# A chunked attention feeding a top-2 expert layer, on one core: first loads and turns reordered, some copies moved between ACT and DVE, routing constants spread over three iterations

## The chip, the cores and the metric

The kernel runs on one core of a Trainium2 chip. A core has a matrix engine (PE, with its weight loads PEld), a vector engine (DVE), a scalar engine (ACT), a general engine (POOL) and a sync engine (SP). Each engine works through its own instructions in order and waits on semaphores that others raise. Loads are queued by an engine and carried by 16 DMA engines. The metric is the device time of one execution in microseconds; lower is better.

## The reference, cut to what matters

Attention works in chunks of 32 queries. Each chunk sees 8 memory keys, up to 16 keys to its left, its own 32 and up to 8 to its right. The rows of the result go through a router with two choices out of 8 experts, each expert being two matrix products with a ReLU between them.

```python
batch, n_heads, seq, head_dim = (4, 8, 768, 64)
chunk, left_ctx, right_ctx = (32, 16, 8)
for c in range(nc):
    k_full = np.concatenate([mem_k, k_ctx], axis=2)
    v_full = np.concatenate([mem_v, v_ctx], axis=2)
    scores = scale * np.matmul(q_c, k_full.transpose(0, 1, 3, 2))
    a = np.exp(scores - np.max(scores, axis=-1, keepdims=True))
    a = a / (np.sum(a, axis=-1, keepdims=True) + 1e-09)
    out[:, :, c_start:c_end] = np.matmul(a, v_full)
...
x = attn_out.transpose(0, 2, 1, 3).reshape(B * S, H * D)        # 3072 rows of 512
noisy_logits = x @ w_gate + np.log1p(np.exp(x @ w_noise)) * noise
top2 = np.argpartition(-noisy_logits, 2, axis=1)[:, :2]
...
h = np.maximum(x[mask] @ w1[e], 0.0)                            # 512 to 1024
out[mask] += top2_w[mask, k, None] * (h @ w2[e])                # 1024 to 512
```

## The kernel before

The attention part takes two heads at a time, a pair: 16 pairs (NPAIR), four of them (HP) for each of the 4 batches. Everything about one pair is a row of short steps, each a function of the pair's number:

- `load_qk(n)` and `load_v(n)` (L126, L134) bring a pair's q, k and v from memory, cast to bf16. All of them are queued on POOL, in program order. q and k have six buffers each (NQ), v has four (NV). A v buffer is cleared once at the start (L161, L166), as chunks at the sequence's ends leave parts of it unwritten. A v load is two transfers, one for each head (three where the first or last head is in it).
- `turn_pe(n, 0)` transposes q on PE (twelve transposes, L254) into one of three PSUM banks, which all transposes share in a ring, and ACT copies the result out (qT, L258). `turn_pe(n, 1)` does k; ACT copies it in two halves (kT, L264) into one of two buffers whose other halves were set to zero (L204).
- `scores_pe` (L273 to L283) multiplies q with the memory keys (mkT) and with the windows of k, into bankS.
- `max_dve` takes the row maxima (mx, L288) and subtracts them (sd, L290), both on DVE. `exp_act` (L295) exponentiates on ACT.
- `PT_pe` transposes the probabilities on PE, `PT_copy` (L307) copies them out on ACT, `PV_pe` (L314, L317) multiplies them with the memory values (memv) and with v, into bankO, and `mult_dve` (L328, L329) divides by the row sums on DVE.
- `xT_pe` transposes the finished rows and copies them out on ACT (xt, L342), and `logits_pe` (L350) multiplies them with the gate weights (wgn).

The order of the work is written by hand: a main loop over i runs PT, PV and the division for pair i - 1, maximum and exponential for pair i, the turns for pair i + 2, the transposes of rows for pair i - 2, and the scores for pair i + 1. It also queues the loads of q and k for pair i + 6 and of v for pair i + 3. So the text below says "iteration i" and means the stretch that begins with pair i's maximum. Ahead of the loop stand the turns of pairs 0 and 1 and the scores of pair 0.

From iteration 6 on, whenever four pairs make a batch complete, the steps of the router (`route`, a list of small functions, put into `pending`) are worked off two at a time, one in the middle and one at the end of each iteration (`steps(1)`). The router needs constants: ramps, identities and small masks, which `route_constants` (L218 to L232) makes on DVE, all of them in iteration 1. The memory keys are transposed by PE ahead of everything else (L241), with a 32x32 identity in fp32 that DVE copies (L194), and ACT copies the result to mkT (L243). At the start ACT holds nothing else but a table load and the issue of the memory keys.

After the loop come the last batch's router, gathers of rows by expert (L615), and the experts' products (`up`, L667; `down`, L683), whose results are scattered to the output (L695). That part is the same in both kernels.

Of the kernel before, what the change touches and what calls it, by code (L numbers as in the profile page):

```python
# [24 lines left out]
def kernel(  # L25
# [14 lines left out]
    nc = tc.nc  # L40
# [48 lines left out]
    def body():  # L89
# [32 lines left out]
        def load_qk(n):  # L122
            b, h0 = divmod(2 * n, H)
            qks[n] = [ap_.tile([128, 2, SJ * D], BF16, name=nm, bufs=NQ) for nm in ("qg", "kg")]
            for dst, src in zip(qks[n], (q, k)):
                nc.gpsimd.dma_start(out=dst, in_=src[b, h0:h0 + 2].rearrange("h (p j) d -> p h (j d)", p=128))  # L126
# [32 lines left out]
        OW = D + 2  # L159
        memv = ap_.tile([128, NPAIR, 2, OW], BF16, name="memv", bufs=1)  # L160
        nc.vector.memset(vbufs[0], 0.0)  # L161
        nc.vector.memset(memv, 0.0)
# [30 lines left out]
        ident = ap_.tile([32, 32], F32, name="ident", bufs=1)  # L193
        nc.vector.tensor_copy(ident, identb[:32, :32])  # L194
        onesb = const.tile([128, 128], BF16, name="onesb")
        nc.vector.memset(onesb, 1.0)
        neg = const.tile([128, 2, left_ctx], BF16, name="neg")
        nc.vector.memset(neg, NEG)
        mkT = ap_.tile([128, HP, B, 2, n_mem], BF16, name="mkT", bufs=1)
        nc.vector.memset(mkT, 0.0)  # L200
        kbufs = [ap_.tile([128, 2, S], BF16, name=f"kT{i}", bufs=1) for i in range(2)]
        for kb in kbufs:
            for hh in range(2):
                nc.vector.memset(kb[64 * (1 - hh):64 * (1 - hh) + 64, hh, :], 0.0)  # L204
# [10 lines left out]
        wgn = rp.tile([128, KP, 2 * E], BF16, name="wgn")  # L215

        def route_constants():
            nc.vector.tensor_copy(ramp, ramp_i)  # L218
            nc.vector.tensor_scalar(out=rampm, in0=ramp_i, scalar1=-128.0, scalar2=None, op0=Alu.add)
            nc.vector.tensor_copy(tokv[:, :NP // 2], tok_i[:, :NP // 2])  # L220
            nc.vector.tensor_scalar(out=tokv[:, NP // 2:], in0=tok_i[:, NP // 2:], scalar1=1.0, scalar2=None, op0=Alu.add)
            nc.vector.tensor_copy(step, step_i)
            nc.vector.memset(ones16, 1.0)
            nc.vector.tensor_copy(ident16, identb)
            for hh in range(2):
                nc.vector.tensor_copy(fold[:, hh, :], identb[:64, :64])
            nc.vector.memset(row0, 0.0)
            nc.vector.memset(row0[0:1, :], 1.0)
            for hh in range(2):
                nc.vector.memset(halfc[64 * hh:64 * hh + 64, :], float(hh))  # L230
                nc.vector.memset(pick[:, hh, :], float(hh))
            nc.vector.tensor_copy(wgn, wgn_f.rearrange("p k t e -> p k (t e)"))  # L232
# [6 lines left out]
        p_m = f32v(tr(), HP, B * n_mem)  # L239
        for hp in range(HP):  # L240
            nc.tensor.transpose(out=p_m[:, hp, :], in_=mk_nat[:, 2 * hp:2 * hp + 2, :].rearrange("p h d -> p (h d)"), identity=ident)  # L241
        for hh in range(2):
            nc.scalar.copy(mkT[64 * hh:64 * hh + 64, :, :, hh, :], p_m[64 * hh:64 * hh + 64].rearrange("p h (b m) -> p h b m", m=n_mem))  # L243


        st = [dict() for _ in range(NPAIR)]
        xrows = {}

        def turn_pe(n, x):
            src = qks[n][x]  # L250
            p_t = bf16v(tr(), SJ, 128)
            for j in range(SJ):
                for hh in range(2):
                    nc.tensor.transpose(out=p_t[64 * hh:64 * hh + 64, j, :], in_=src[:, hh, j * D:(j + 1) * D], identity=identb)  # L254
            p_t = p_t.rearrange("d j p -> d p j")
            if x == 0:
                dst = ap_.tile([128, 128, SJ], BF16, name="qT", bufs=2)
                nc.scalar.copy(dst, p_t)  # L258
                st[n]["qT"] = dst.rearrange("d p j -> d (p j)")
            else:  # L260

                for hh in range(2):
                    hs = slice(64 * hh, 64 * hh + 64)
                    nc.scalar.copy(kbufs[n % 2][hs, hh].rearrange("d (p j) -> d p j", j=SJ), p_t[hs])  # L264

        UB = BT // 2

# [18 lines left out]
        def max_dve(n):  # L286
            mx = ap_.tile([128, 2, BT], F32, name="mx")
            nc.vector.tensor_reduce(out=mx, in_=st[n]["ps"], axis=AX, op=Alu.max)  # L288
            sd = ap_.tile([128, 2, BT, CTX], F32, name="sd", bufs=1)
            nc.vector.tensor_tensor(out=sd, in0=st[n]["ps"], in1=mx.rearrange("p x (u o) -> p x u o", o=1).to_broadcast([128, 2, BT, CTX]), op=Alu.subtract)  # L290
            st[n]["sd"] = sd
# [10 lines left out]
                nc.tensor.transpose(out=p_p[:, u, :], in_=P[:, u, :, :], identity=identb)  # L302
            st[n]["p_p"] = p_p

        def PT_copy(n):
            PT = ap_.tile([128, BT, 128], BF16, name="PT", bufs=1)
            nc.scalar.copy(PT, st[n]["p_p"])  # L307
            st[n]["PT"] = PT

        def PV_pe(n):  # L310
# [543 lines left out]

        PT_pe(n - 1)
        max_dve(n)
        PT_copy(n - 1)
        PV_pe(n - 1)
        exp_act(n)
# [180 lines left out]
```

## Time and profile before

| | us |
|---|---|
| median of 3 runs | 334.99 |
| lowest and highest run | 334.16, 338.81 |
| the profiled execution, device time | 335.06 |
| its span, first to last instruction | 333.0 |
| PE, DVE, ACT, POOL busy | 271.9, 163.0, 149.5, 227.4 |

The profile is one execution, with a start and a duration in us for each instruction, counted from the start of the span; 2.06 us of the execution lie outside it. In a timeline row the numbers are start and duration, then engine, line, operation, written tile and read tile, shapes, the count of instructions merged into the row, and in brackets how long the engine stood idle before it and what released it. In a window row they are the length of the stretch and the busy time of each engine in it. For a group of instructions they are the busy sum, the mean duration in ns, and the idle time ahead of it. For a load they are its size and the time from issue to landing. Most of the idle time of ACT and DVE in the expert part is theirs to have, since PE is the busy engine there.

### The profile page before, as it was taken

Reading aid. Unit: us, or ns where it says so; the run is one execution under the profiler, and the core shown is the slowest. Engines: PE = TensorE matmul, PEld = TensorE weight load, DVE = VectorE, ACT = ScalarE, POOL = GpSimd, SP = SyncE. Lnnn points to the kernel's source line nnn. Section 1 sums busy time; section 2 is a strip of 40 time slices with the busy share of each in tenths; the row PEclk is TensorE's granted clock in tenths of the full one; section 3 lists DMA queues with packets and bytes.
Section 4 is the critical chain, followed back from the end, with each engine's and each line's share of the span. In section 5 each row is a group of like instructions: output and inputs, shape, how many; then the busy total and the mean of one; then the engine's idle time right before and its main releaser. Section 6 shows DMA issues by size and latency. Waiting matters only on the chain.

```text
span 333.0 us, 7629 instructions
## 1 busy us (share of the span) xinstructions
PE 271.9 (82%) x3065; PEld 173.2 (52%) x3085; DVE 163.0 (49%) x363; ACT 149.5 (45%) x295; POOL 227.4 (68%) x220
## 2 busy tenths in 40 slices
PE   0776777786766768969999999999999999999920
PEld 0655565565655557536546464564554556455410
DVE  7556668869998684313434342342342434234200
ACT  1687997788673644313343423323422324333100
POOL 8996878554652256774878686887886888675480
PEclk9978997989875799999999999999999999999975
DMA  9999999999997998899989999999999979979293
GB/s 106 157 150 186 171 162 165 213 140 151 237 213 160 335 362 291 132 220 248 172 162 196 210 204 200 211 174 198 190 208 214 183 122 173 196 86 134 33 130 49
DMA packets 99846, 60.30 MB, mean 181 GB/s; under 512 B 65056, under 2 KB 84768, under 8 KB 99808
## 3 DMA queue, kind: packets, MB, share of 16 engines
q0 software_dynamic: 82160, 50.63, 106.8%
q1 hardware_dynamic: 14272, 8.98, 9.2%
q10 hardware_dynamic: 3376, 0.16, 1.0%
q8 instruction: 26, 0.43, 0.5%
q14 instruction: 12, 0.10, 0.1%
HBM read 65.07 MB, written 23.27 MB: 265 GB/s over the span
## 4 chain that ended last, share of the span: by engine, by line
PE 45%; DVE 15%; issue 13%; DMA 8%; ACT 8%; POOL 8%; POOLq 1%; DVEq 0%; ACTq 0%
PE bankE L683 13%; PE bankE L667 12%; POOL out_dram L695 7%; PE bankT L667 6%; DMA out_dram<-ys,idx_h 4%; DMA w2t<-in_moe_w_dram 3%; ACT kT L264 3%; DVE xrow L329 2%; PE bankO L314 2%; PE bankO L317 2%; PE bankT L638 2%; ACT PT L307 2%; PE bankT L254 2%; DVE mx L288 2%; DVE Rn L454 2%
## 5 line engine op out<-in xcount | busy, mean ns | idle before, releaser
L695 POOL DMA_INDIRECT out_dram<-ys,idx_f x40 | 63.1, 1577 | 24.0 <-issue 16.3
L667 PEld LDWEIGHTS <-w1t 128*128 128x128 bf16 x576 | 55.2, 99 | 36.4 <-issue 5.0
L683 PE MATMUL bankE<-w2t,htf 128*128 128x512 bf16 x278 | 64.7, 379 | 0.5
L615 POOL DMA_INDIRECT xl<-x_rows,idx_f x48 | 50.0, 1041 | 22.2 <-issue 10.1
L694 DVE TENSOR_SCALAR ys<-bankE,gt 128x512 f32<-128x512 f32 (+1 forms) x32 | 21.9, 684 | 63.8 <-PE bankE L683 50.8
L667 PE MATMUL bankE<-xTf,w1t 128*128 128x320 bf16 (+1 forms) x250 | 51.3, 338 | 1.7 <-ACT xTf L640 1.4
L692 ACT ACTIVATE ys<-bankE,gt 128x512 f32<-128x512 f32 x24 | 16.5, 688 | 65.5 <-PE bankE L683 51.7
L134 POOL DMA_DIRECT2D vp<-in_v_dram x34 | 33.3, 986 | 15.5 <-PE bankO L317 4.4
L683 PEld LDWEIGHTS <-htf 128*128 128x128 bf16 x288 | 27.4, 97 | 29.9 <-issue 0.2
L652 DVE TENSOR_SCALAR htf<-bankE 128x512 bf16<-128x512 f32 (+1 forms) x32 | 18.9, 592 | 28.3 <-PE bankE L667 28.3
L650 ACT ACTIVATE htf<-bankE 128x512 bf16<-128x512 f32 (+1 forms) x32 | 16.5, 517 | 27.5 <-PE bankE L667 26.4
L264 ACT COPY kT<-bankT 64x768 bf16<-64x768 bf16 x32 | 25.3, 791 | 6.3 <-PE bankT L254 6.1
L667 PE MATMUL bankT<-xTf,w1t 128*128 128x320 bf16 (+1 forms) x128 | 27.8, 339 | 0.0
L683 PE MATMUL bankE<-w2t,hts 128*128 128x512 bf16 x92 | 21.5, 379 | 2.8 <-DMA w2t<-in_moe_w_dram 2.6
L638 PEld LDWEIGHTS <-xl 128*128 128x128 bf16 (+1 forms) x224 | 15.5, 99 | 12.4 <-issue 4.7
L638 PE MATMUL bankT<-identb,xl 128*128 128x128 bf16 (+1 forms) x224 | 20.3, 218 | 0.8 <-ACT xt L342 0.5
L667 PE MATMUL bankE<-xTs,w1t 128*128 128x256 bf16 (+1 forms) x128 | 18.8, 290 | 2.2 <-ACT xTs L640 1.4
L314 PE MATMUL bankO<-memv,PT 128*128 128x132 bf16 x96 | 10.3, 258 | 12.3 <-ACT PT L307 8.0
L288 DVE TENSOR_REDUCE mx<-bankS 128x12 f32<-128x768 f32 x16 | 15.2, 953 | 8.9 <-PE bankS L283 8.8
L652 DVE TENSOR_SCALAR htf<-bankT 128x512 bf16<-128x512 f32 (+1 forms) x16 | 9.5, 592 | 15.3 <-PE bankT L667 14.4
L290 DVE TENSOR_TENSOR sd<-bankS,mx 128x768 f32<-128x768 f32 x16 | 15.3, 958 | 1.9 <-ACT xt L342 0.5
L295 ACT ACTIVATE P<-sd 128x768 bf16<-128x768 f32 x16 | 13.6, 850 | 5.3 <-DVE sd L290 5.3
(182 smaller groups left out, 449.3 us busy)
## 6 DMA issues: line engine op xcount, KB each, us to landing
w1t<-in_moe_w_dram POOLq DMA_DIRECT2D x8, 1024.0 KB, 12.4
w2t<-in_moe_w_dram POOLq DMA_DIRECT2D x8, 1024.0 KB, 11.2
out_dram<-zt SPq DMA_DIRECT2D x3, 2048.0 KB
vp<-in_v_dram POOLq DMA_DIRECT2D x30, 168.0 KB, 7.8
qg<-in_q_dram POOLq DMA_DIRECT2D x16, 192.0 KB, 7.8
kg<-in_k_dram POOLq DMA_DIRECT2D x16, 192.0 KB, 8.2
x_rows<-xrow SPq DMA_DIRECT2D x2, 792.0 KB, 9.0
x_rows<-xrow SPq DMA_DIRECT2D x1, 768.0 KB, 8.3
```

The costliest lines, as they stand in the source:

```text
L134: nc.gpsimd.dma_start(out=vp[p0 + j:p0 + j + nj, c:c + m, hh, :], in_=bass.AP(v.tensor, v.offset + (hd * S + c * chunk + j - left_ctx) * D ...
L264: nc.scalar.copy(kbufs[n % 2][hs, hh].rearrange("d (p j) -> d p j", j=SJ), p_t[hs])
L288: nc.vector.tensor_reduce(out=mx, in_=st[n]["ps"], axis=AX, op=Alu.max)
L314: nc.tensor.matmul(out=pv[:, u // UB, u % UB], lhsT=PT[:, u, :], rhs=memv[:, n], start=(u % UB == 0), stop=False, skip_group_check=True)
L615: nc.gpsimd.indirect_dma_start(out=xl, out_offset=None, in_=xd[:upto], in_offset=bass.IndirectOffsetOnAxis(ap=idx[:, c:c + 1], axis=0), bo ...
L638: nc.tensor.transpose(out=p_t[:, kp, :w], in_=xl[:w, kp * 64:(kp + 1) * 64].bitcast(BF16), identity=identb[:w, :w])
L650: nc.scalar.activation(out=dst, in_=src, func=Act.Relu)
L652: nc.vector.tensor_scalar(out=dst, in0=src, scalar1=0.0, scalar2=None, op0=Alu.max)
L667: nc.tensor.matmul(out=h[:, :hi - lo], lhsT=W1[e][:, kp, f * 128:(f + 1) * 128], rhs=xTs[s][:, kp, lo:hi], start=(kp == 0), stop=(kp == KP ...
L683: nc.tensor.matmul(out=y, lhsT=ht[:, f, o:o + w], rhs=W2[e][:, f, :], start=(f == 0), stop=(f == FB - 1))
L694: nc.vector.tensor_scalar(out=ys[:, :wide], in0=y[:, :wide], scalar1=gate, scalar2=None, op0=Alu.mult)
L695: ins = nc.gpsimd.indirect_dma_start(out=rows, out_offset=bass.IndirectOffsetOnAxis(ap=idx, axis=0), in_=ys[:, :wide], in_offset=None, bou ...
```

## The change

The order of the first instructions is new on every engine:

- POOL queues q and k of pair 2 ahead of v of pair 0, makes the router's index tables ahead of the loads of pair 3, and queues v of pairs 1 and 2 behind q and k of pairs 3 and 4. v of pair 3 moves out of the start altogether: iteration 0 queues it, after q and k of pair 6.
- DVE clears one v buffer, then the memory keys' tile and the halves of the two kT buffers, then makes the identity and the other small constants, and only then clears memv and the last v buffer. The second and third v buffer are cleared by ACT, which copies the first one's zeros.
- PE turns q of pair 0 first, then the memory keys, then k of pair 0 and q of pair 1; the scores of pair 0 stand ahead of k of pair 1. For pairs 0 and 2 one of the two halves of kT is copied by DVE instead of ACT.

In the loop, the maximum and the subtraction become two functions, and in iterations 1 to 6 DVE copies PT between them (pairs 0 to 5); from iteration 7 on ACT copies PT as before. The router's constants become six entries of `pending`, which iterations 0 to 2 work off, two in each.

```diff
         nc.vector.memset(vbufs[0], 0.0)
+        mkT = ap_.tile([128, HP, B, 2, n_mem], BF16, name="mkT", bufs=1)
+        nc.vector.memset(mkT, 0.0)
+        kbufs = [ap_.tile([128, 2, S], BF16, name=f"kT{i}", bufs=1) for i in range(2)]
+        for kb in kbufs:
+            for hh in range(2):
+                nc.vector.memset(kb[64 * (1 - hh):64 * (1 - hh) + 64, hh, :], 0.0)
+        ident = ap_.tile([32, 32], F32, name="ident", bufs=1)
+        nc.vector.tensor_copy(ident, identb[:32, :32])
...
-        for vb in vbufs[1:]:
-            nc.vector.memset(vb, 0.0)
+        flat = lambda t: t.rearrange("p c h d -> p (c h d)").bitcast(F32)
+        for vb in vbufs[1:3]:
+            nc.scalar.copy(flat(vb), flat(vbufs[0]))
+        nc.vector.memset(vbufs[3], 0.0)
+        load_qk(2)
         load_v(0)
...
-        load_qk(2)
-        load_v(1)
-        load_qk(3)
...
+        load_qk(3)
+        load_v(1)
+        load_qk(4)
         load_v(2)
-        load_qk(4)
-        load_v(3)
         load_qk(5)
...
         def route_constants():
...
+            return [
+                (lambda: V.tensor_copy(wgn, wgn_f.rearrange("p k t e -> p k (t e)")), lambda: V.tensor_copy(step, step_i)),
+                (lambda: V.tensor_copy(ramp, ramp_i), lambda: V.memset(ones16, 1.0)),
+                (lambda: V.tensor_scalar(out=rampm, in0=ramp_i, scalar1=-128.0, scalar2=None, op0=Alu.add), lambda: V.tensor_copy(ident16, identb)),
...
+                (halves,),
+                (folds,)]
...
-        def turn_pe(n, x):
+        def turn_pe(n, x, both=False):
...
-                    nc.scalar.copy(kbufs[n % 2][hs, hh].rearrange("d (p j) -> d p j", j=SJ), p_t[hs])
+                    (nc.vector.tensor_copy if both and hh else nc.scalar.copy)(kbufs[n % 2][hs, hh].rearrange("d (p j) -> d p j", j=SJ), p_t[hs])
...
-        def PT_copy(n):
+        def PT_copy(n, copy=nc.scalar.copy):
             PT = ap_.tile([128, BT, 128], BF16, name="PT", bufs=1)
-            nc.scalar.copy(PT, st[n]["p_p"])
+            copy(PT, st[n]["p_p"])
...
-        for n in range(2):
-            turn_pe(n, 0)
-            turn_pe(n, 1)
-            if n == 0:
-                scores_pe(0)
+        turn_pe(0, 0)
+        memory_keys()
+        turn_pe(0, 1, True)
+        turn_pe(1, 0)
+        scores_pe(0)
+        turn_pe(1, 1)
+        pending.extend(route_constants())
         for i in range(NPAIR - 1):
...
             max_dve(i)
-            if i >= 1:
+            if 1 <= i <= HP + 2:
+                PT_copy(i - 1, nc.vector.tensor_copy)
+            sub_dve(i)
+            if i > HP + 2:
                 PT_copy(i - 1)
...
-                turn_pe(i + 2, 1)
+                turn_pe(i + 2, 1, i == 0)
...
-            if 1 <= i <= NPAIR - NV:
+            if i <= NPAIR - NV:
                 load_v(i + NV - 1)
-            if i == 1:
-                route_constants()
```

`memory_keys` is the old code of L241 and L243 as a function, `folds` and `halves` the old lines for the masks, `sub_dve` the old L290.

More of the change, by code (lines that the diff above doesn't have):

```diff
@@ L161, in body @@
         nc.vector.memset(vbufs[0], 0.0)
+        mkT = ap_.tile([128, HP, B, 2, n_mem], BF16, name="mkT", bufs=1)
[6 more added lines that the diff above has]
+        nc.vector.tensor_copy(ident, identb[:32, :32])
+        onesb = const.tile([128, 128], BF16, name="onesb")
+        nc.vector.memset(onesb, 1.0)
+        neg = const.tile([128, 2, left_ctx], BF16, name="neg")
+        nc.vector.memset(neg, NEG)
         nc.vector.memset(memv, 0.0)
@@ L186, in body @@
         nc.gpsimd.affine_select(out=tie, in_=tie, compare_op=Alu.is_gt, fill=0.0, base=0, pattern=[[1, E], [-1, E]], channel_multiplier=0)
+        load_qk(3)
+        load_v(1)
+        load_qk(4)
         load_v(2)
-        load_qk(4)
-        load_v(3)
         load_qk(5)
[L193 to L204, printed above, removed]
         ramp = const.tile([128, 128], F16, name="ramp")
@@ L217, in route_constants, with halves, folds @@
         def route_constants():
[L218 to L232, printed above, removed]
+            V = nc.vector
+            def halves():
+                for hh in range(2):
+                    V.memset(halfc[64 * hh:64 * hh + 64, :], float(hh))
+                    V.memset(pick[:, hh, :], float(hh))
+            def folds():
+                for hh in range(2):
+                    V.tensor_copy(fold[:, hh, :], identb[:64, :64])
+                V.memset(row0, 0.0)
+                V.memset(row0[0:1, :], 1.0)
+            return [
+                (lambda: V.tensor_copy(wgn, wgn_f.rearrange("p k t e -> p k (t e)")), lambda: V.tensor_copy(step, step_i)),
+                (lambda: V.tensor_copy(ramp, ramp_i), lambda: V.memset(ones16, 1.0)),
+                (lambda: V.tensor_scalar(out=rampm, in0=ramp_i, scalar1=-128.0, scalar2=None, op0=Alu.add), lambda: V.tensor_copy(ident16, identb)),
+                (lambda: V.tensor_copy(tokv[:, :NP // 2], tok_i[:, :NP // 2]),
+                 lambda: V.tensor_scalar(out=tokv[:, NP // 2:], in0=tok_i[:, NP // 2:], scalar1=1.0, scalar2=None, op0=Alu.add)),
+                (halves,),
+                (folds,)]
         seen = rp.tile([128, E], F16, name="seen")
@@ L237, in body @@
         tabs = [rp.tile([128, NC_], F32, name=f"tab{i}") for i in range(2)]
[L239 to L243, printed above, removed]
         st = [dict() for _ in range(NPAIR)]
         xrows = {}
-        def turn_pe(n, x):
+        def turn_pe(n, x, both=False):
             src = qks[n][x]
@@ L263, in turn_pe, with memory_keys @@
                     hs = slice(64 * hh, 64 * hh + 64)
-                    nc.scalar.copy(kbufs[n % 2][hs, hh].rearrange("d (p j) -> d p j", j=SJ), p_t[hs])
+                    (nc.vector.tensor_copy if both and hh else nc.scalar.copy)(kbufs[n % 2][hs, hh].rearrange("d (p j) -> d p j", j=SJ), p_t[hs])
+        def memory_keys():
+            p_m = f32v(tr(), HP, B * n_mem)
+            for hp in range(HP):
+                nc.tensor.transpose(out=p_m[:, hp, :], in_=mk_nat[:, 2 * hp:2 * hp + 2, :].rearrange("p h d -> p (h d)"), identity=ident)
+            for hh in range(2):
+                nc.scalar.copy(mkT[64 * hh:64 * hh + 64, :, :, hh, :], p_m[64 * hh:64 * hh + 64].rearrange("p h (b m) -> p h b m", m=n_mem))
         UB = BT // 2
@@ L856, in body @@
         max_dve(n)
+        sub_dve(n)
         PT_copy(n - 1)
```

3 lines of the change are left out of this document (added).

## The prediction

> **What bounds the kernel now.** I read the page first: the span, the busy shares, the row of PE in forty slices of 8.3 us.
>
> ```profile
> span 333.0 us, 7629 instructions
> ...
> PE 271.9 (82%) x3065; PEld 173.2 (52%) x3085; DVE 163.0 (49%) x363; ACT 149.5 (45%) x295; POOL 227.4 (68%) x220
> ...
> PE   0776777786766768969999999999999999999920
> ```
>
> From the nineteenth slice on (about 150 us) PE is full: the expert stage, which the change does not touch. Every edit lies in the attention stage ahead of it, where PE has gaps in each slice, and what that stage gains moves the rest forward as a block, because its first transfers and gathers are released by the attention's results. So the sum is made at the start of each head pair's maximum on DVE (L288), the one instruction per iteration that follows the scores. I write mx(i) for it; iteration i of the loop begins there. The windows between six of these starts are next: us, then busy time of each engine, granted clock, DMA share (over 1 where packets of one engine overlap), GB/s.
>
> ```profile
> 17.54:24.97 7.43, 5.29 (x110) 4.06 (x110) 4.48 (x20) 6.29 (x9) 7.03 (x11) 0.77 1.69 145
> ...
> 28.04:34.95 6.91, 4.93 (x107) 3.94 (x106) 3.11 (x6) 5.64 (x8) 5.64 (x7) 0.75 1.66 182
> 34.95:39.51 4.56, 3.56 (x107) 2.90 (x106) 3.10 (x5) 4.21 (x7) 4.07 (x6) 1.00 1.89 169
> 39.51:44.56 5.05, 3.78 (x107) 2.99 (x106) 3.10 (x4) 4.70 (x7) 4.00 (x5) 1.00 1.84 174
> 44.56:51.50 6.94, 3.84 (x106) 3.05 (x105) 4.54 (x8) 6.03 (x10) 3.43 (x4) 1.00 2.39 157
> ```
>
> Iterations 4 and 5 are the steady state: ACT is busy 4.21 of 4.56 and 4.70 of 5.05 us, so ACT bounds them. Iterations 1 and 3 are long (7.43 and 6.91) for other reasons, which the timeline gives below. The loads never stop: 145 to 182 GB/s in every window.
>
> **The start.** The timeline of the first 14 us, and two loads with their time to landing (first q, then k, of pair 0):
>
> ```profile
> 1.18 1.34 DVE L161 MEMSET vp<- 128x1536 uint32 x1 [1.18 <-PEq L1024]
> ...
> 8.82 0.12 DVE L194 CAST ident<-identb 32x32 f32<-32x32 bf16 x1
> ...
> 9.00 0.63 PE L241 MATMUL bankT<-ident,mk_nat 32*128 32x32 f32 x4 [9.00 <-DVE ident L194]
> ...
> 9.40 1.88 DVE L204 MEMSET kT<- 64x384 uint32 x4
> ...
> 9.56 0.85 PE L254 MATMUL bankT<-identb,qg 128*64 128x128 bf16 x12
> ...
> 12.81 0.29 PE L280 MATMUL bankS<-kT,qT 128*32 128x80 bf16 x4 [1.18 <-ACT kT L264]
> ...
> 13.62 0.96 DVE L288 TENSOR_REDUCE mx<-bankS 128x12 f32<-128x768 f32 x1 [2.34 <-PE bankS L283]
> ```
>
> ```profile
> 1.36 0.92 POOL L126 DMA_DIRECT2D qg<-in_q_dram  x1 [0.85 <-POOLq L1024]
> 2.27 0.81 POOL L126 DMA_DIRECT2D kg<-in_k_dram  x1
> ```
>
> ```profile
> qg<-in_q_dram POOLq DMA_DIRECT2D x1, 192.0 KB, 4.2
> ```
>
> ```profile
> kg<-in_k_dram POOLq DMA_DIRECT2D x1, 192.0 KB, 5.5
> ```
>
> PE's first instruction waits until 9.00 for a 32x32 identity that DVE reaches only after four large memsets, though q landed at 1.36 + 4.2 = 5.6 and k at 2.27 + 5.5 = 7.8. The change puts q's turn first, which needs no identity of DVE's, and the small DVE constants behind one memset. The new chain: k at 7.8, its turn 0.85 (as the row at 9.56), 8.65; then the two halves of the kT copy side by side, on ACT and on DVE; then the scores, 13.62 - 12.81 = 0.81. DVE's half has no row, so it goes between rows:
>
> ```profile
> L642 DVE COPY xTf<-bankT 128x512 bf16<-128x512 bf16 x18 | 7.5, 415 | 2.6 <-PE bankT L638 2.6
> ...
> L642 DVE COPY xTf<-bankT 128x256 bf16<-128x256 bf16 x6 | 1.7, 280 | 0.0
> ```
>
> ```profile
> L264 ACT COPY kT<-bankT 64x768 bf16<-64x768 bf16 x32 | 25.3, 791 | 6.3 <-PE bankT L254 6.1
> ...
> L307 ACT COPY PT<-bankT 128x768 bf16<-128x768 bf16 x16 | 12.8, 802 | 3.0 <-PE bankT L302 2.9
> ...
> L640 ACT COPY xTf<-bankT 128x512 bf16<-128x512 bf16 x18 | 10.5, 583 | 9.4 <-PE bankT L638 9.4
> ```
>
> By 415 at 512 and 280 at 256 elements a contiguous DVE copy of 768 takes 0.55 us. The kT half reads with a stride, so I take the 0.96 of mx, which reads as many elements one at a time; then mx(0) = 8.65 + 0.96 + 0.81 + handovers = 10.5, against 13.62: 3.1 earlier. With 0.55 ACT's half (0.79) sets it and the gain is 3.3. The other end: the memory keys (mk_nat) may land late. PE used them at 9.00, so they landed by then; if exactly then, 9.00 + 0.63 + 0.85 + 0.96 + 0.81 = 12.3, and the gain is 1.3. I take 3.1, since nothing shows mk_nat as a releaser.
>
> Costed at nothing here: the two v buffers that ACT copies. By ACT's 583 and 802 a copy of 1536 fp32 elements is 1.45 us, an estimate; two of them from 2.5 end near 5.5, before ACT's first copy at about 6.5. Their cover is ACT's idle start. The v load into the buffer they read waits for them, and POOL, which now issues pair 2's q and k first, comes to it near 6.5 too. DVE's own list, the memset of 1.34, the kT memsets of 1.88 and the small ones, reaches the identity near 5 and its last memset near 8.3, before the kT half at 8.65.
>
> **Iterations 0 to 3 are paced by the loads.** Timeline rows, then the time to landing of the three loads of q (pair 4), q (pair 5) and k (pair 6), issued at 17.76, 21.16 and 23.75.
>
> ```profile
> 17.76 0.75 POOL L126 DMA_DIRECT2D qg<-in_q_dram  x1
> ...
> 19.18 2.02 POOL L134 DMA_DIRECT2D vp<-in_v_dram  x2
> ...
> 21.16 0.77 POOL L126 DMA_DIRECT2D qg<-in_q_dram  x1
> ...
> 23.39 0.49 DVE L218 CAST ramp<-ramp_i 128x128 f16<-128x128 int32 x1
> ...
> 23.75 0.77 POOL L126 DMA_DIRECT2D kg<-in_k_dram  x1
> ...
> 23.70 0.21 PE L283 MATMUL bankS<-neg,onesb 128*32 128x16 bf16 x1
> ...
> 24.97 0.95 DVE L288 TENSOR_REDUCE mx<-bankS 128x12 f32<-128x768 f32 x1
> ...
> 30.27 0.53 PE L254 MATMUL bankT<-identb,qg 128*64 128x128 bf16 x12 [1.85 <-DMA qg<-in_q_dram]
> ...
> 34.95 0.96 DVE L288 TENSOR_REDUCE mx<-bankS 128x12 f32<-128x768 f32 x1 [1.14 <-PE bankS L283]
> ```
>
> ```profile
> qg<-in_q_dram POOLq DMA_DIRECT2D x1, 192.0 KB, 6.6
> ```
>
> ```profile
> qg<-in_q_dram POOLq DMA_DIRECT2D x1, 192.0 KB, 9.1
> ```
>
> ```profile
> kg<-in_k_dram POOLq DMA_DIRECT2D x1, 192.0 KB, 9.4
> ```
>
> Two things made these iterations long. The routing constants keep DVE from 23.39 to mx(2) at 24.97, 1.58 us; spread, they go under waits. And PE waits 1.85 us at 30.27 for q of pair 5. That wait is what remains: a start 3.1 earlier asks for it 3.1 earlier, and spreading the constants earlier still. It landed at 21.16 + 9.1 = 30.3. In the new order v of pair 3 goes behind q and k of pairs 5 and 6, so the two transfers of 19.18 no longer stand ahead. What they are worth: q of pair 4 landed at 17.76 + 6.6 = 24.4, so 5.9 us passed for k, two v pieces and q; k of pair 6 landed at 23.75 + 9.4 = 33.15, so the three loads after q of pair 5 took 2.9, 0.96 each. Two of these off 5.9 leave 4.0 for v. If only POOL's issue counted it would be 2.0 (the row at 19.18). I take 2.9, between them, since both queues are full: q of pair 5 at 27.4. From there to mx(4) PE worked without a gap, 34.95 - 30.27 = 4.68, and does so again; mx(4) comes at 32.05, 2.9 earlier. So of the 3.1 of the start nearly all is kept, but the constants' 1.58 and the wait's 1.85 are not gained on top of it.
>
> **Iterations 4 to 6: PT on DVE.**
>
> ```profile
> 35.93 0.80 ACT L307 COPY PT<-bankT 128x768 bf16<-128x768 bf16 x1
> ...
> 36.79 0.52 PE L314 MATMUL bankO<-memv,PT 128*128 128x132 bf16 x6 [1.00 <-ACT PT L307]
> ...
> 39.51 0.96 DVE L288 TENSOR_REDUCE mx<-bankS 128x12 f32<-128x768 f32 x1 [0.48 <-PE bankS L283]
> ...
> 51.12 0.32 PE L280 MATMUL bankS<-kT,qT 128*32 128x112 bf16 x11 [2.00 <-issue]
> ```
>
> ACT loses 0.80 per iteration and has 3.4 to 3.9 left, so it ceases to bound. What is late next is a ring: mx 0.96, PT on DVE 0.55, two handovers of 0.06 (36.79 less 35.93 + 0.80), then from PV to the next mx 39.51 - 36.79 = 2.72: 4.35 us. The subtraction, queued behind PT, runs beside PV, and the exponential that waits for it has until the next iteration. Against 4.56 and 5.05 (mean 4.80) that is 0.45 per iteration. The same ring with a copy of 0.96 gives 4.76, no gain. And v limits it: v of pair 3, now last of the same set of transfers, lands where the last of them landed, 33.15 or a little later; PV(3) wants it at 32.05 + 0.96 + 0.55 + 0.12 = 33.7. With half a microsecond of room and the loads at 0.96 per q or k and up to 4.0 per v pair, I credit 0.2 of the 0.45, three times: 0.6 (0 to 1.35).
>
> From iteration 7 PT is ACT's again and only the block moves.
>
> **Sum.** 2.9 + 0.6 = 3.5 us. The profiled execution took 335.06, its span 333.0; 335.06 - 3.5 = 331.5. The median of the runs shown is 334.99, 0.07 below it.
>
> **Rivals.** *The loads do not bind.* Were the early wait of PE an accident of issue order, start, constants (the scores of pair 2 end at 23.70 + 0.21, so 24.97 - 23.91 = 1.05), the 1.85 and three times 0.45 would add: 3.1 + 1.05 + 1.85 + 1.35 = 7.35, 327.7. For it: DMA share 1.66 to 1.69 in the windows with the waits against 1.89 after. Against: times to landing that grow from 6.6 to 9.4 while POOL issues without a pause. Chance 0.17.
>
> *The loads take all.* If v of pair 3 costs the next sets what it saved q, and iterations 4 to 6 wait for v, only the 0.5 of a shorter tail stays: 334.5. For it: 4.0 for a v pair plus 1.9 is more than an iteration of 4.80. Chance 0.14.
>
> *Half clock.* In the window from 17.54 the granted clock is 0.77, which is 2 x 0.23 x 7.43 = 3.4 us at half speed; twelve turns then take 0.85 instead of 0.53, so such a stretch costs up to 3.4 x (1 - 0.53/0.85) = 1.3. PE would wait for q of pairs 3, 4 and 5; two more stretches give 331.5 + 2.6 = 334.1. The Trainium skill, "TensorE: Matmul & The Clock Gate", section on HAM oscillation, says that a matmul loop that waits on DMA falls back to half clock again and again; here only the two long windows of those shown, 1 and 3, carry it, so the trace agrees so far. Chance 0.06.
>
> *Slower: PE's instructions come late.* At 51.12 PE had stood 2.00 us on "issue" in the middle of the scores, in the window with the highest DMA share, 2.39; nothing that the profile tracks released it. If denser loads bring such stops into iterations 0 to 6, where the profile shows none before 49 us, each costs 2.0; from the second on the gain is gone, three give 331.5 + 6.0 = 337.5. Against: the share is 1.66 to 1.89 in the other windows without a stop. Chance 0.07.
>
> **Numbers.** Forecast 0.53, rivals 0.17, 0.14, 0.06, 0.07, 0.03 for what I do not see. The forecast's own bounds are gains of 1.3 (mk_nat late, no tail) and 3.3 + 1.35 = 4.65, times of 333.8 and 330.4. The range 327.5 to 335.8 takes these in, the load and clock rivals, and about half of the first; out are half of that, the stops and the rest, 0.18. A measurement of this kernel tells some 2% from no change: 328.3 and 341.7. Faster than that only in the first rival and not in all of it: 0.14; slower only with five or more stops or something unseen: 0.05; within: 0.81.
>
> **What would show it.** Right: PE's first instruction near 5.7; mx(0) near 10.5; PE waiting on q of pairs 4 or 5; mx(4) near 32; PT on DVE at 0.55 and windows of 4.4 to 4.7 after it; the attention's end and the first expert matmuls about 3.5 earlier, and the chain after them unchanged. Wrong: mx(2) to mx(4) without a wait for a load (then nearer 328); PV waiting for v in iterations 4 to 6, or PT near 0.96 (then 332 to 334.5); any new PE stop on "issue" before 49 us.

## The result, and the profile after

| | before | after |
|---|---|---|
| median, us | 336.81 (4 runs, 334.16 to 338.81) | 332.28 (4 runs, 330.15 to 332.96) |
| ratio, 95% interval | | 0.9887 (0.9837 to 0.9936) |
| the profiled execution, span | 335.06, 333.0 | 332.96, 331.2 |

The changed kernel is 1.1% faster (0.6 to 1.6%), 3.8 us of 336.81; the two medians themselves lie 4.5 apart. Ratios, and the means of profiles further down, leave out executions more than 1.5% above the fastest of their kernel. The forecast was 331.5 with a range of 327.5 to 335.8, and no change that 2% can tell: time and range held. Of the steps behind it several did not.

The page of the changed kernel, its span, busy shares and the row of PE in forty slices:

```profile
span 331.2 us, 7638 instructions
...
PE 274.2 (83%) x3065; PEld 174.3 (53%) x3085; DVE 166.5 (50%) x369; ACT 147.3 (44%) x289; POOL 227.6 (69%) x220
...
PE   2768677768666777799979999999999999999960
```

PE is still full in the expert stage; the gaps are still in the attention. The windows between the starts of pairs 0 to 6, columns as before:

```profile
11.44:18.14 6.70, 3.82 (x86) 3.20 (x86) 4.09 (x8) 4.61 (x6) 6.64 (x9) 0.91 1.82 144
18.14:23.00 4.86, 3.38 (x76) 2.72 (x77) 3.98 (x10) 1.73 (x3) 4.54 (x7) 0.50 1.75 152
23.00:26.96 3.96, 3.69 (x101) 2.96 (x100) 3.78 (x13) 3.12 (x5) 2.90 (x5) 0.90 1.50 194
26.96:31.16 4.20, 3.62 (x107) 2.99 (x106) 3.48 (x6) 3.98 (x6) 3.27 (x4) 1.00 1.99 167
31.16:36.71 5.55, 3.81 (x107) 3.04 (x106) 3.48 (x6) 3.94 (x6) 3.79 (x5) 1.00 1.90 172
36.71:42.47 5.76, 3.79 (x107) 2.99 (x106) 3.51 (x5) 5.10 (x7) 4.17 (x6) 1.00 1.99 168
```

mx(0) comes at 11.44 instead of 13.62, mx(4) at 31.16 instead of 34.95. But iteration 0 is long now (6.70 against 3.92), and iterations 4 and 5, forecast at 4.4 to 4.7, take 5.55 and 5.76 with PE at full clock; in iteration 4 no engine is busy for more than 3.94 of 5.55. The timeline shows both. First the start and the two pairs whose kT is split between ACT and DVE:

```profile
2.56 2.84 ACT L179 COPY vp<-vp 128x1536 f32<-128x1536 f32 x2 [0.49 <-DVE vp L161]
...
5.93 0.85 PE L255 MATMUL bankT<-identb,qg 128*64 128x128 bf16 x12 [5.93 <-DMA qg<-in_q_dram]
...
8.79 0.79 ACT L265 COPY kT<-bankT 64x768 bf16<-64x768 bf16 x1 [0.75 <-PE bankT L255]
...
9.62 0.96 DVE L265 COPY kT<-bankT 64x768 bf16<-64x768 bf16 x1 [1.55 <-ACT kT L265]
...
16.10 0.96 DVE L265 COPY kT<-bankT 64x768 bf16<-64x768 bf16 x1 [2.53 <-ACT kT L265]
...
17.07 1.02 DVE L234 CAST ramp<-ramp_i 128x128 f16<-128x128 int32 x1
...
18.14 0.96 DVE L296 TENSOR_REDUCE mx<-bankS 128x12 f32<-128x768 f32 x1
...
19.01 0.55 DVE L319 COPY PT<-bankT 128x768 bf16<-128x768 bf16 x1
...
19.61 0.84 PE L326 MATMUL bankO<-memv,PT 128*128 128x132 bf16 x6 [2.94 <-DVE PT L319]
```

DVE's half of kT begins when ACT's half ends (8.79 + 0.79 = 9.58), not beside it: it waits for ACT, as the bracket says. For pair 2 that half stands on DVE ahead of mx(1), whose scores PE had ended at 14.36, and behind mx(1) stands PT, for which PE waits 2.94 us. Then the places where PE stood on "issue" (nothing that the profile tracks released it) in iterations 4 to 6:

```profile
34.71 0.24 PE L329 MATMUL bankO<-vp,PT 128*32 128x128 bf16 x4 [1.16 <-issue]
...
41.46 0.40 PE L352 MATMUL bankT<-identb,xrow 128*128 128x128 bf16 x4 [1.36 <-issue]
...
46.83 0.33 PE L288 MATMUL bankS<-kT,qT 128*32 128x112 bf16 x11 [0.33 <-issue]
```

Before had one such stop up to the end of its iteration 6, 2.00 at 51.12.

### The profile page after: what moved, and what is told of

The parts are those of the page before. It is cut to its first block, busy times and chain, and to the rows that moved or that the text cites. A ratio compares the mean times of both kernels' runs of the same rounds, so it can differ in the third digit from the quotient of the medians.

```text
span 331.2 us, 7638 instructions
## 1 busy us (share of the span) xinstructions
PE 274.2 (83%) x3065; PEld 174.3 (53%) x3085; DVE 166.5 (50%) x369; ACT 147.3 (44%) x289; POOL 227.6 (69%) x220
## 4 chain that ended last, share of the span: by engine, by line
PE 53%; DVE 13%; DMA 12%; issue 9%; POOL 5%; ACT 4%; POOLq 1%; DVEq 0%; ACTq 0%
PE bankE L695 20%; PE bankE L679 13%; PE bankT L679 7%; POOL out_dram L707 3%; PE bankT L650 3%; DMA w1t<-in_moe_w_dram 3%; DMA vp<-in_v_dram 3%; DMA out_dram<-ys,idx_h 3%; DMA qg<-in_q_dram 2%; DVE Rn L466 2%; PE bankT L255 2%; DMA kg<-in_k_dram 2%; PE bankE L701 2%; DVE xrow L341 1%; PE bankS L288 1%
## 5 line engine op out<-in xcount | busy, mean ns | idle before, releaser
L265 ACT COPY kT<-bankT 64x768 bf16<-64x768 bf16 x30 | 23.7, 791 | 7.9 <-PE bankT L255 7.5
L255 PE MATMUL bankT<-identb,qg 128*64 128x128 bf16 x192 | 10.0, 248 | 8.3 <-DMA qg<-in_q_dram 6.5
```

Of the source, the lines that this page charges most:

```text
L265: (nc.vector.tensor_copy if both and hh else nc.scalar.copy)(kbufs[n % 2][hs, hh].rearrange("d (p j) -> d p j", j=SJ), p_t[hs])
```

## The experiments

After the result the theory was that the new start is the whole gain, and that PT on DVE, the split of kT and the spread constants are worth nothing. The rivals were that each of these carries a part, and, within the start, that the load order alone or the order of the first turns alone would do. Ratios are against the kernel before, timed on the same chip, with 95% intervals.

**Both kernels once more,** to see how far one profiled execution carries.

> The changed kernel as it is, a second profile. Theory A (the gain is made in the first eight iterations and what happens later varies from run to run with the granted clock and with stops of PE on issue): the starts of the maximum repeat up to the fourth within 0.3 us (11.4, 18.1, 23.0, 27.0, 31.2), but the stops and the half-clock stretches lie elsewhere, and the start of the sixteenth differs from 97.5 by 1 us or more. Rival B (the later loss belongs to the change): the sixteenth starts at 97 to 98 again. Time 331 to 333 by both.

> The kernel before as it is, a second profile, to see how far one profiled execution stands for the median. Theory A (the first profile was a fast one): the starts of the maximum repeat for the first four within 0.3 us (13.6, 17.5, 25.0, 28.0), the last one and the first copy of expert rows on ACT (97.0 and 108.4) come 1 to 3 us later. Rival B: they repeat within 0.5 us, and the change's gain is made behind the attention. Time 335 to 338.

After: 333.92, 0.9885 (0.9833 to 0.9937). Before against itself: 336.07, 0.9971 (0.9932 to 1.001). The gain repeats; the starts do so less closely than expected. In the changed kernel mx(1) came at 17.20 and mx(4) at 30.43, 0.94 and 0.73 earlier than in its first profile, with the stops at the same three places; in the kernel before the last start came 0.6 earlier instead of later. In the second execution of before PE has no wait for q of pair 5, and iteration 3 looks like this:

```profile
28.39:33.70 5.31, 3.61 (x107) 2.98 (x106) 3.10 (x4) 4.95 (x8) 4.98 (x7) 1.00 1.76 180
```

5.31 instead of 6.91, for the same instructions: at a granted clock of 1.00 instead of 0.75 PE needs 3.61 instead of 4.93. So 1.6 us of the iteration that the prediction built on, in which PE alone was busy 1.32 longer, belonged to that one execution.

**The start alone:** the changed kernel without PT on DVE and with all constants in iteration 1 again; turns, load order and the split of kT stay.

```diff
-        pending.extend(route_constants())
...
-            if 1 <= i <= HP + 2:
-                PT_copy(i - 1, nc.vector.tensor_copy)
...
-            if i > HP + 2:
+            if i >= 1:
                 PT_copy(i - 1)
...
+            if i == 1:
+                for fns in route_constants():
+                    for fn in fns:
+                        fn()
```

> The changed kernel with PT on ACT throughout and all routing constants at the end of iteration 1: of the change only the new start is left (order of loads and turns, v buffers by ACT, halves of kT on DVE). Theory A (the start makes the whole gain): ratio 0.985 to 0.993. Rival B (the constants have to be spread for it to be kept, 1.58 us of DVE ahead of the third maximum): ratio 0.993 to 1.0, mx(2) 1 us or more later than with the constants spread (20.7).

332.44, 0.9899 (0.9858 to 0.9941). The start carries the gain, as far as these intervals tell.

**Its two halves apart.** First the new load order in the kernel before, nothing else:

```diff
+        load_qk(2)
         load_v(0)
...
-        load_qk(2)
-        load_v(1)
-        load_qk(3)
...
+        load_qk(3)
+        load_v(1)
+        load_qk(4)
         load_v(2)
-        load_qk(4)
-        load_v(3)
...
-            if 1 <= i <= NPAIR - NV:
+            if i <= NPAIR - NV:
                 load_v(i + NV - 1)
```

> The kernel before with the new order of the loads and nothing else. Theory A (the loads pace iterations 2 and 3; v of pair 3 behind q and k of pair 5 brings them forward): the wait of PE for q of pair 5 (1.85 us at 30.3) goes or shrinks below 0.5, mx(4) 1.5 to 3 us earlier than 34.95, ratio 0.990 to 0.996. Rival B (the turns and the identity at the start make the gain): mx(4) earlier by less than 1 us, ratio 0.997 to 1.003.

336.01, 0.9998 (0.9963 to 1.0033): no gain that shows. Yet the wait at 30.27 is gone. Its timeline in iteration 3, and that window (this profiled execution took 340.59 us; its first four starts lie within 0.23 of before's):

```profile
27.86 1.58 ACT L263 COPY kT<-bankT 64x768 bf16<-64x768 bf16 x2
...
29.46 0.80 ACT L341 COPY xt<-bankT 128x768 bf16<-128x768 bf16 x1
...
30.16 0.81 ACT L306 COPY PT<-bankT 128x768 bf16<-128x768 bf16 x1
...
31.02 0.52 PE L313 MATMUL bankO<-memv,PT 128*128 128x132 bf16 x6 [1.00 <-ACT PT L306]
...
34.98 0.96 DVE L287 TENSOR_REDUCE mx<-bankS 128x12 f32<-128x768 f32 x1 [1.41 <-PE bankS L282]
```

```profile
28.12:34.98 6.86, 4.88 (x106) 4.05 (x105) 3.10 (x5) 5.83 (x8) 5.21 (x7) 0.75 2.13 163
```

ACT's queue of kT, xt and PT holds PV until 31.02. The same place in the timeline of the kernel before, behind the turn of q of pair 5 that had waited:

```profile
30.07 0.80 ACT L307 COPY PT<-bankT 128x768 bf16<-128x768 bf16 x1
...
30.93 0.83 PE L314 MATMUL bankO<-memv,PT 128*128 128x132 bf16 x6
```

There the turn ended at 30.27 + 0.53 = 30.80 and ACT's PT at 30.87, so PV could not have begun earlier: the wait of 1.85 for q cost nothing. The second profile of before shows the same without that wait:

```profile
29.46 0.53 PE L254 MATMUL bankT<-identb,qg 128*64 128x128 bf16 x12 [0.69 <-ACT kT L264]
...
30.98 0.52 PE L314 MATMUL bankO<-memv,PT 128*128 128x132 bf16 x6 [1.00 <-ACT PT L307]
```

Then the new order of DVE's and PE's first work in the kernel before, with the old loads:

```diff
-        for n in range(2):
-            turn_pe(n, 0)
-            turn_pe(n, 1)
-            if n == 0:
-                scores_pe(0)
+        turn_pe(0, 0)
+        memory_keys()
+        turn_pe(0, 1)
+        turn_pe(1, 0)
+        scores_pe(0)
+        turn_pe(1, 1)
```

(with the identity and masks behind one memset, and two v buffers copied by ACT, as in the change)

> Kernel before with the new order of DVE's and PE's first work alone (identity, memory keys and masks behind one memset, two v buffers by ACT, q of pair 0 turned first); loads in the old order, the routing constants in iteration 1, PT and all of kT on ACT. Theory A (the earlier first turn is the whole gain): mx(0) near 11.1, mx(1) below 15 as in the kernel with kT on ACT, ratio to before near 0.990, 333. Theory B (the early start needs the early q and k of pair 2): PE waits 1 us or more for q or k of pair 2, mx(1) at 16 or later, mx(4) within 1 us of before's 34.95, ratio 0.995 to 1.000.

336.03, 0.9997 (0.9962 to 1.0032): no gain that shows either. The timeline, POOL's issues of v of pair 0 and q of pair 2, then PE's turn of that q:

```profile
5.70 2.67 POOL L134 DMA_DIRECT2D vp<-in_v_dram  x3 [0.62 <-ACT vp L179]
...
9.56 0.75 POOL L126 DMA_DIRECT2D qg<-in_q_dram  x1
...
10.98 0.96 DVE L297 TENSOR_REDUCE mx<-bankS 128x12 f32<-128x768 f32 x1 [2.91 <-PE bankS L292]
...
14.19 0.85 PE L256 MATMUL bankT<-identb,qg 128*64 128x128 bf16 x12 [2.49 <-DMA qg<-in_q_dram]
...
17.05 0.96 DVE L297 TENSOR_REDUCE mx<-bankS 128x12 f32<-128x768 f32 x1 [4.12 <-PE bankS L292]
```

mx(0) is 2.64 earlier, mx(1) only 0.49: PE waits 2.49 for q of pair 2, queued at 9.56 behind v of pair 0 and the memory values. Further on it waits 1.83 for q of pair 3 (at 19.58) and 1.79 for q of pair 5 (at 29.98).

**Both halves, without the rest.** PT and kT all on ACT in the changed kernel (its constants stay spread):

```diff
-        turn_pe(0, 1, True)
+        turn_pe(0, 1)
...
-            if 1 <= i <= HP + 2:
-                PT_copy(i - 1, nc.vector.tensor_copy)
...
-            if i > HP + 2:
+            if i >= 1:
                 PT_copy(i - 1)
...
-                turn_pe(i + 2, 1, i == 0)
+                turn_pe(i + 2, 1)
```

> Changed kernel with PT and both halves of kT on ACT in every iteration; new start, new load order and spread constants stay. Theory A (PT and kT on DVE are worth nothing together): mx(1) near 14.4, iterations 4 to 6 at 4.6 to 5.0, a ratio of 0.988 to 0.991, as the changed kernel. Rival (they help each other, DVE taking from ACT what bounds iterations 2 to 6): ratio 0.994 or above, mx(4) at 31.5 or later.

333.08, 0.9887 (0.9835 to 0.9939), the changed kernel's ratio. A second form has PT on DVE in iterations 3 to 6 only:

```diff
-            if 1 <= i <= HP + 2:
+            if 3 <= i <= HP + 2:
                 PT_copy(i - 1, nc.vector.tensor_copy)
...
-            if i > HP + 2:
+            if 1 <= i < 3 or i > HP + 2:
                 PT_copy(i - 1)
```

(with kT all on ACT)

> Changed kernel with kT all on ACT, and PT on DVE only in iterations 3 to 6, where ACT was the busiest engine; PT on ACT in iterations 1 and 2. Theory A (loads and stops bind there whatever engine copies PT): mx(1) near 14.4, waits of PE for q or v of 0.5 to 1.8 us in iterations 2 to 5, mx(7) at 46 to 47.5, ratio 0.988 to 0.992. Rival (PT on DVE pays once mx(1) is no longer late): mx(7) at 44 or below and a ratio of 0.985 or less.

333.02, 0.9885 (0.9835 to 0.9935). Its timeline, POOL and PE, pairs 1 and 2:

```profile
5.06 0.72 POOL L126 DMA_DIRECT2D qg<-in_q_dram  x1
...
6.49 2.67 POOL L134 DMA_DIRECT2D vp<-in_v_dram  x3
...
11.51 0.85 PE L255 MATMUL bankT<-identb,qg 128*64 128x128 bf16 x12
...
14.02 0.96 DVE L296 TENSOR_REDUCE mx<-bankS 128x12 f32<-128x768 f32 x1 [0.54 <-PE bankS L291]
```

The same turn of q of pair 2 runs at 11.51 without a wait. The starts and lengths of the first iterations side by side:

| | mx(0) | it. 0 | it. 1 | it. 2 | it. 3 | mx(4) |
|---|---|---|---|---|---|---|
| before | 13.62 | 3.92 | 7.43 | 3.07 | 6.91 | 34.95 |
| before, again | 13.63 | 3.67 | 7.72 | 3.37 | 5.31 | 33.70 |
| load order alone | 13.84 | 3.93 | 7.29 | 3.06 | 6.86 | 34.98 |
| turns alone | 10.98 | 6.07 | 7.66 | 3.10 | 6.85 | 34.66 |
| both, PT late on DVE | 11.00 | 3.02 | 6.64 | 4.11 | 4.56 | 29.33 |
| the changed kernel | 11.44 | 6.70 | 4.86 | 3.96 | 4.20 | 31.16 |

Each half by itself gives 0.9997 or 0.9998; the seven kernels with both, those told below included, give 0.9885 to 0.9928. It is not a sum of parts. No run has both halves and nothing else: the start alone keeps the split of kT, the kernel with PT and kT on ACT keeps the spread constants.

**PT on DVE:** taken out of the changed kernel, and put by itself into the kernel before (out: the two hunks of the start's diff that concern `PT_copy`). In:

```diff
-            if i >= 1:
+            if 1 <= i <= HP + 2:
+                PT_copy(i - 1, nc.vector.tensor_copy)
+            sub_dve(i)
+            if i > HP + 2:
                 PT_copy(i - 1)
```

> The changed kernel with PT copied by ACT in all iterations, after the subtraction as before. Theory A (the ring of maximum, PT on DVE, PV and scores makes an iteration 4.2 us where ACT made it 4.8): iterations without a stop take 4.6 to 5.0 us again, mx(7) comes 2 to 3.5 us later than 47.8; time 1 to 3 us over the changed kernel. Rival B (v and the loads limit iterations 4 to 6): the iterations stay under 4.5 or PV waits for v; time within 0.7 us.

> The kernel before with PT on DVE in iterations 1 to 6 and nothing else of the change. Theory A: the wait for q of pair 5 near 30.3 stays, iterations 4 to 6 shrink to 4.2 to 4.4 us where PE has no stop, mx(7) at 49.5 to 50.5 instead of 51.5; time 1 to 2 us under before. Rival B (the loads limit): no gain at mx(7), time within 0.7 us of before.

Out: 332.77, 0.9887 (0.9843 to 0.9932). In: 336.52, 0.9994 (0.9957 to 1.0031). No gain from it shows in either time, though the intervals are wide enough to hide 1 us. Without it mx(7) came at 47.32, where 2 to 3.5 us later than 47.8 had been expected. One iteration of the kernel before with PT on DVE, and the wait ahead of it:

```profile
24.46 0.85 PE L254 MATMUL bankT<-identb,qg 128*64 128x128 bf16 x12 [2.38 <-DMA qg<-in_q_dram]
```

```profile
29.27:33.47 4.20, 4.20 (x107) 3.36 (x106) 3.47 (x5) 3.39 (x6) 3.67 (x6) 0.82 1.74 180
```

The iteration in the second fence, number 3, is even below the prediction's ring of 4.35. But the loads are no faster for it: with the old order PE waits 2.38 for q in iteration 2, which takes 5.89 instead of 3.07.

**kT all on ACT,** PT on DVE as in the change:

```diff
-        turn_pe(0, 1, True)
+        turn_pe(0, 1)
...
-                turn_pe(i + 2, 1, i == 0)
+                turn_pe(i + 2, 1)
```

> The changed kernel with both halves of kT of pairs 0 and 2 on ACT, as before the change. Theory A (the two halves do not run side by side, DVE's waits for ACT's, so the split only puts 0.96 us and a wait into DVE's queue ahead of the second maximum): mx(0) within 0.3 us of 11.4, mx(1) near 14.5 instead of 18.1, and later starts earlier by up to 2 us; time 0 to 2 us under the changed kernel. Rival B (the loads pace iterations 1 to 3): mx(1) moves, mx(3) and mx(4) stay within 0.3 us of 27.0 and 31.2, PE waits for q or k instead; time the same.

334.14, 0.992 (0.9874 to 0.9966). Its timeline, mx(1) and the waits that follow:

```profile
14.32 0.96 DVE L296 TENSOR_REDUCE mx<-bankS 128x12 f32<-128x768 f32 x1 [0.84 <-PE bankS L291]
...
26.21 0.53 PE L255 MATMUL bankT<-identb,qg 128*64 128x128 bf16 x12 [1.81 <-DMA qg<-in_q_dram]
...
32.20 0.55 PE L329 MATMUL bankO<-vp,PT 128*32 128x128 bf16 x24 [0.82 <-DMA vp<-in_v_dram]
```

mx(1) is 3.8 earlier than in the changed kernel (18.14): 0.4 of it stood at mx(0) already (11.07 against 11.44), the rest is mostly the second split half on DVE and the long cast behind it. The time does not follow: PE now waits 1.81 and 0.82 for q and v. The first of these is a real loss, since PT for the PV behind it was ready at 25.56. At mx(4) 1.8 of the 3.8 is left (29.39 against 31.16), and at mx(7) 0.6 (47.21 against 47.80), behind two stops on "issue" of 1.63 and 1.57.

**The constants in iteration 1,** all else as changed (the first and the last hunk of the start's diff).

> The changed kernel with all routing constants at the end of iteration 1, PT on DVE as changed. Theory A (spreading them is worth nothing, as in the changed kernel they delay the second maximum by a microsecond instead of the third): mx(1) near 16.5 to 17 instead of 17.2 to 18.1, mx(2) within 1 us of 22 to 23, time within 0.5% of the changed kernel. Rival B: 1 to 2 us slower.

333.93, 0.9928 (0.9888 to 0.9967): the interval overlaps the changed kernel's, so a gain from spreading them is not shown. Its profile is the one with PT on DVE and no stop on "issue" of 0.2 us or more before 74 us. Iterations 4 to 6 take 4.58, 4.23 and 5.32 there, 14.13 in all, against 16.64 in the changed kernel, 16.55 in the kernel before and 16.11 in the start alone, which has PT on ACT and a stop of 1.24. At mx(15) this lead is gone (95.55 against 94.93 in the start alone).

**Without the loads of v from pair 4 on.** This leaves out 12 of 16 v loads; the products run on what the buffers hold.

```diff
-            if i <= NPAIR - NV:
+            if i == 0:
                 load_v(i + NV - 1)
```

> Changed kernel that leaves out the loads of v for pairs 4 to 15; their products run on what the buffers hold. Theory A (PE's stops on issue in iterations 4 to 6 and the late steps come with dense loads): no stop of 0.5 us or more before 60, iterations 4 to 8 at 4.2 to 4.6, the first copy of expert rows 3 us or more before the changed kernel's 107.89, ratio 0.98 or below. Rival (they belong to PE's own stream of instructions, or to the clock): one to three stops of 1 us or more between 34 and 60 as before, and a ratio of 0.985 to 0.99.

331.29, 0.9865 (0.9793 to 0.9937), no resolvable gain over the changed kernel, though the first copy of gathered expert rows comes at 103.69 instead of 107.89, as the theory of dense loads had it. (Its rows can be routed otherwise, so the expert part need not be the same work.) PE's stops in it:

```profile
33.99 0.24 PE L329 MATMUL bankO<-vp,PT 128*32 128x128 bf16 x4 [0.37 <-issue]
...
39.92 0.40 PE L352 MATMUL bankT<-identb,xrow 128*128 128x128 bf16 x4 [0.53 <-issue]
...
45.56 0.32 PE L288 MATMUL bankS<-kT,qT 128*32 128x112 bf16 x11 [0.60 <-issue]
```

They stand ahead of the same three groups of instructions as in the changed kernel, but take 1.50 in all instead of 1.16 + 1.36 + 0.33 = 2.85, and iterations 4 and 5 take 4.76 and 4.94 instead of 5.55 and 5.76. So these places do not depend on the loads of v; that their size grows with the transfers is what these two executions suggest, not more: the third stop is the longer one without the loads. Nor do they stop every execution: with the constants in iteration 1 none of the three shows. What causes them stays open.

## Why the prediction was right, and where its steps were not

**The start.** Right in kind, 0.9 too large: mx(0) came 2.2 earlier, not 3.1. The copies of kT "side by side, on ACT and on DVE" run one after the other, 0.79 and then 0.96, and end 1.79 after the first began; both on ACT take 1.61. DVE's half was priced right, at 0.96; the order was not looked at. The Trainium skill, "PSUM — Partial Sum Buffer", section "PSUM bank collisions raise a hardware error", advises guarding PSUM by bank and quadrant (32 partitions), and calls guarding by bank the simple version. The halves lie on different partitions of one bank, and the wait at 9.62 agrees with the simple version; whether they could run together no run here shows. The two halves also share the written tile, but that alone need not order them: in the kernel before ACT and DVE copy into one xTf tile at the same time (from 162.93 for 0.59 and from 163.15 for 0.41), out of two PSUM tiles. Halves in two PSUM tiles were not tried. The fear that mk_nat would be late fell: with q turned first, PE waited at most 0.26 us for the memory keys in any kernel that does so. ACT's v buffers took 2.84 for two against an estimate of 2.9, and what waited on them was at most a v load, 0.62 us in the kernel with the turns alone.

**"Iterations 0 to 3 are paced by the loads."** This is the step that failed, though its number came out near: mx(4) 3.8 earlier against 2.9, and 2.5 against the second profile of before. The wait at 30.27 does not set mx(4): with the load order alone it goes and mx(4) stays at 34.98, because PT comes from ACT's queue at the same time. And in the changed kernel PE waits for no load from mx(2) to mx(4), which the prediction had named as a sign against itself. The turn of q of pair 5 waits for ACT instead:

```profile
27.71 0.53 PE L255 MATMUL bankT<-identb,qg 128*64 128x128 bf16 x12 [0.38 <-ACT kT L265]
```

From it to mx(4) 3.45 us pass, not the 4.68 that the prediction carried over from an iteration with a granted clock of 0.75. So 27.71 was met (27.4), by another releaser, and the stretch behind it was 1.2 too long. What the load order does is elsewhere and earlier. It brings q of pair 2 (issued at 5.06, where the kernel with the turns alone has 9.56) to a PE that now asks for it at 11.5. Without that most of the earlier turns' gain is lost by mx(1) (0.49 of 2.64 is left); without the earlier turns nobody needs it. The prediction moved `load_qk(2)` ahead of `load_v(0)` without pricing it, and gave the credit to v of pair 3. Which of the load moves matter was not run apart; in the kernel with the turns alone the 2.49 us wait points to pair 2, the 1.83 behind it to pair 3. Where mx(1) is early, as with kT on ACT, the loads do bind for a time.

**Iterations 4 to 6.** The ring was right: PT on DVE 0.55, an undisturbed iteration of 4.20 against 4.35 forecast. The 0.6 credited does not show in the time: the two ratios with and without PT on DVE are 0.9887 and 0.9887, and in the kernel before it gives 0.9994, with intervals too wide to exclude 0.6. In the changed kernel's profile iterations 4 to 6 gain nothing (16.64 against 16.55), with stops on "issue" of 2.85 against 2.00; where no stop came they took 14.13, and that lead was lost later. In iteration 1 PT on DVE stands behind a late maximum (19.01 behind 18.14).

**The constants** were to bring nothing of their own; nothing is shown.

**The rivals.** *The loads do not bind*: right about the wait at 30.27, which cost nothing and which the second profile of before does not have; its sum, which adds that wait as a gain, was not met, as no kernel with both halves and all its loads has a median below 332.28, against 327.7. *The loads take all*: the median is 2.2 below its 334.5, and in the changed kernel PE waits for no v in iterations 4 to 6; no row shows the 0.5 for a shorter tail that it keeps. *Half clock*: its price was right. The same iteration of the same kernel took 4.93 of PE at 0.75 and 3.61 at 1.00, 1.32 apart; but such stretches occur in both kernels, and move from one execution to the next (for where they fell, see the tail). No wait for a load is needed for one: with the load order alone iteration 3 has 0.75 without it. *PE stops on issue*: they came, three before 49 us, which the prediction had named as a sign against itself. In sum they were not new: stops of 0.3 us or more up to the attention's end add to 3.89 in the changed kernel and 3.27 in the kernel before, and to 4.10 in the second profile of the latter.

**The tail.** "Moves the rest forward as a block" holds for the expert part at most, not for the second half of the attention. Four profiles with at most one half of the new start (before twice, turns alone, before with PT on DVE) and six with both (changed, start alone, constants at once, PT on ACT, kT on ACT, PT late) have these means, in us:

| | mx(8) | mx(9) | mx(12) | mx(15) | first copy of gathered expert rows | device time |
|---|---|---|---|---|---|---|
| at most one half | 56.2 | 62.6 | 78.9 | 97.5 | 108.4 | 334.8 |
| both | 52.3 | 59.5 | 76.5 | 95.9 | 106.7 | 333.2 |
| earlier by | 3.9 | 3.1 | 2.4 | 1.6 | 1.7 | 1.5 |

So more than half of the gain is lost between mx(8) and mx(15); what is left at the expert rows reaches the end. In the two profiles shown mx(15) is even later, 97.46 against 96.99, where the prediction expected the attention's end about 3.5 earlier. One thing in the windows goes with the loss: length times (1 - granted clock), summed over the iterations, is 3.3 us ahead of mx(8) and 8.3 behind it with both halves, 5.6 and 4.9 with at most one (an estimate from the window rows). So in these profiles the stretches at a lower clock lie later where the start is earlier; that they cause the loss was not tested. Single executions of one group differ by 2 us and more, and the ratios of the timed runs give gains of 0.7 to 1.2%, 2.4 to 3.9 us.

So that the time came out is in part luck: a start 0.9 too good, a PT gain that does not show and a block that shrinks stood against a gain by mx(4) that was forecast too small and from another cause. The base was low as well, 335.06 for the profiled execution against a median of 336.81 beside the changed kernel (and 335.06 - 3.5 is 331.56, not 331.5).

## What to carry to other kernels

When a change lets an engine start earlier, follow each of its next inputs to the place in the queue where it is issued: here the early turns and the new load order show no gain apart and 2.4 to 3.9 us together. A wait in the profile is worth its length only if nothing else ends just behind it; look for what is second, here ACT's copy of PT, 0.07 us behind the turn that had waited. And before splitting one copy over two engines, see in a profile whether the halves run together; here, read from one PSUM tile, the second half was queued, not parallel.

## What the runs showed of the hardware that was not expected

- Two engines reading different partitions of one PSUM tile ran in turn in every kernel that split kT (8.79 to 9.58 on ACT, 9.62 on DVE).
- The same DVE cast of 128x128 from int32 to f16 took 0.22 us in some executions and 1.02 at 17.07 in the changed kernel, while POOL was issuing a v load; in its second profile the cast ran beside the same issue in 0.23, so that alone does not make it long. The cause was not tested.
- An execution's time goes with its mean granted clock: over the runs that the ratios use, with a constant for each kernel, 0.01 of clock more goes with 0.51 us less (95% interval 0.27 to 0.75); over all runs it is 1.01 (0.73 to 1.29). One profiled execution per kernel cannot carry a difference of 1%.
